# A one-element activation ahead of five waiting activations on ScalarE, in a float32 kernel of cross-attention and a gated MLP

## The chip, the cores and the metric

One Trainium2 chip, of which the kernel uses one core. The core has five engines with an instruction stream each: TensorE (PE in the profile, with its weight loads as PEld), VectorE (DVE), ScalarE (ACT), GpSimd (POOL) and SyncE (SP), the last two used here to start DMA transfers. The engines run side by side and wait for each other through semaphores. The metric is the device time of one execution in microseconds (us); lower is better. Inputs and outputs are float32 or float64 arrays in the device's memory (HBM), and the whole computation is one launch.

## The reference

Eight batches of eight heads attend in both directions between 512 tokens and 32 states; the two results are joined into 4352 rows of 512 and go through a gated MLP of width 2048.

```python
B, H, S, Ns, D = (8, 8, 512, 32, 64)            # x: (B,H,S,D)  state: (B,H,Ns,D)
scores = scale * x @ state^T;   a  = softmax(scores, -1);   xread = a  @ state
scores2 = scale * state @ x^T;  a2 = softmax(scores2, -1);  sread = a2 @ x
attn = concatenate([xread, sread], axis=2)      # (B, H, S + Ns, D)
x = attn.transpose(0, 2, 1, 3).reshape(B * (S + Ns), H * D)        # 4352 x 512
h = x @ w_in                                    # 4352 x 2048
sp = np.maximum(h, 0.0) + np.log1p(np.exp(-np.abs(h)))             # softplus
g = h * erf(sp)
return (g @ w_out).astype(np.float32)           # 4352 x 512
```

## The kernel before

Everything stays in float32. The MLP's input is never formed for the tokens: since xread is a @ state, `mixed` (line 841; `mixed0` at 602 for batch 0) multiplies the states of a batch by a part of w_in first, and `first_product` (935) multiplies the result by the transposed attention weights, which gives h transposed. The width of 2048 is worked in two halves (u = 0, 1), the tokens one batch at a time. `first_product` and `second_product` (1020) use seven block products in place of eight with sums of blocks around them (`seven`, 909), and `twice_product` (1123) does so at two levels. Those sums are DVE's work.

Between the two products stands the gate. For each of four blocks of h, ACT copies the block from PSUM into a large buffer called `ring` (line 961) or DVE adds it there (963, 967); ACT makes softplus of it (`soft`, line 971; 633 for batch 0; 1424 for the states), then erf (`serf`, line 986; 638; 1431), and DVE multiplies (989) and makes sums (1000). Attention itself needs the exponential on ACT (`attend`, lines 750 and 753). Softplus, erf and exponential need different function tables on ACT; the table is changed by an instruction of its own, ACT_TABLE_LOAD, which the compiler puts in wherever the next activation needs another table than the one at hand. There are 53 of them in the program. Copies run with any table.

The kernel doesn't issue instructions as it meets them. Each step is recorded with `op(engine, cost, at, go, reads, writes, table, ...)` (line 140), where `go` issues the instructions and `table` names the ACT table, if any. The order on each engine is then written out by hand in `ORDER` (177 to 298), as numbers of the recorded steps of that engine. `emit` (304) walks these five lists with a small model of costs (a change of table is 1.41 there, line 328) to interleave the engines, and calls the `go` of each step in the resulting order; `in_order` (78) then fixes that order on every engine. The waits follow from the data: the framework adds to each instruction the semaphores that it must wait for.

An instruction carries one wait. Where an activation must wait for two engines, the framework puts a separate instruction (EVENT_SEMAPHORE in the trace) ahead of it for the other one. In the built program the table load, where one is needed, stands directly ahead of the activation: ahead of the activation's own wait, and behind the separate one. Five of the 53 loads have such a separate wait ahead of them, all for DVE:

- the 4th load, of the softplus in line 633 (first half of batch 0), and the 8th, of the softplus in the same line (second half);
- the 10th, of the exponential in line 753 (batch 1);
- the 25th, of the softplus in line 971, and the 32nd, in the same line.

The fixed small tiles come from the pool `const`, first in the list of pools; `x`, `xq` (xin), `xT`, `sc` (att), `aT`, `sy` (keep), `m`, `sx` (mix), `raw` (act), `ot` and `oo` (outs) lie in pools that are allocated behind it.

Of the kernel before, what the change touches and what calls it, by code (L numbers as in the profile page):

```python
# [9 lines left out]
F32 = mybir.dt.float32  # L10
U32 = mybir.dt.uint32
ALU = mybir.AluOpType
ACTF = mybir.ActivationFunctionType
# [4 lines left out]
def kernel(  # L18
# [17 lines left out]
    nc = tc.nc  # L36
# [3 lines left out]
    P = 128  # L40
# [11 lines left out]
    const = ctx.enter_context(tc.tile_pool(name="const", bufs=1))  # L52
# [84 lines left out]
    PE, ACT, DVE, SP, GP = "tensor", "scalar", "vector", "sync", "gpsimd"  # L137
    ops, wrote, seen = [], {}, {}

    def op(engine, cost, at, go, reads=(), writes=(), table=None, land=0.0, pipe=0.0):  # L140
        n = len(ops)
        needs = set()
        for r in reads:
            needs.update(wrote.get(r, ()))
        for r in writes:
            needs.update(wrote.get(r, ()))
            needs.update(seen.get(r, ()))
        for r in reads:
            seen.setdefault(r, []).append(n)
        for r in writes:  # L150
            wrote[r], seen[r] = [n], []
        ops.append((engine, cost, at, go, needs, table, land, pipe))
# [5 lines left out]
    def either(name, cost, out, in_, at, reads, writes, by=None, run=None):  # L158
# [15 lines left out]
        else:  # L174
# [122 lines left out]
            36 39 35 38 42 37 44 40-41 43 46-47 52 45 48 55-56 49-50 53 57 51 54 59-60 63-64 61 65  # L297
            58 62 66 70 67 73 69 71 68 72 75 74 77 76 78 80 79 81 83 82""",
    }
    STARTS = {PE: 0.78, ACT: 0.74, DVE: 1.0, SP: 0.74, GP: 1.0}  # L300
    LAG = {PE: 0.24, ACT: 0.16, DVE: 0.17, SP: 0.2, GP: 0.2}
    FIXED, AHEAD = 2.5, 4.0

    def emit():

        mine = {e: [n for n, o in enumerate(ops) if o[0] == e] for e in LAG}
        queue = {}
        for e, text in ORDER.items():
            runs = [[int(k) for k in run.split("-")] for run in text.split()]
            queue[e] = deque(mine[e][k] for r in runs for k in range(r[0], r[-1] + 1))  # L310
            assert sorted(queue[e]) == mine[e]
        free, begin, end, piped = dict(STARTS), {}, {}, 0.0
        loaded = {ACT: None, PE: None}
        while any(queue.values()):
            ready = []
            for e, line in queue.items():
                if line and all(m in end for m in ops[line[0]][4]):
                    n = line[0]
                    ready.append((max([free[e]] + [end[m] + LAG[ops[m][0]] * (
                        ops[m][0] != e or ops[m][7] > 0) for m in ops[n][4]]), n, e))  # L320
            begun, n, e = min(ready)
            queue[e].popleft()
            begin[n] = begun
            _, cost, _, _, _, table, land, pipe = ops[n]
            if e == PE and table != loaded[PE]:
                cost, loaded[PE] = cost + (0.1 if table else 0.26), table
            elif e == ACT and table not in (None, loaded[ACT]):
                cost, loaded[ACT] = cost + 1.41, table
            end[n] = free[e] = begun + cost
            if pipe:  # L330
                piped = max(piped, begun) + pipe
                end[n] = max(piped, free[e]) + (land or FIXED)
                if e == SP:
                    free[e] = max(free[e], piped - AHEAD)
        order = sorted(begin, key=lambda n: (begin[n], n))
        for n in order:
            ops[n][3]()

    def adopt(names, into):

        every = [*names, *into]
        used = sorted({n for r in every for n in [*wrote.get(r, ()), *seen.get(r, ())]})
        for r in every:
            wrote[r], seen[r] = used, []
# [998 lines left out]
    def sums_states(u, at):  # L1343

        def part(j, k):
            return lambda: of_group[2 * u + j][:, :, 2 * k:2 * k + 2, :]

        def spare(k):
            return (mt(3) if k else static["aT0"]).rearrange("p e (i k f) -> p (e i) k f", k=2,
                                                             f=P)  # L1350

        def s4():
            return kept_tile("sx", lambda: mix.tile([P, 3, gw], F32, name="sx", bufs=1))[:, 0:2] \
                .rearrange("p e (i k f) -> p (e i) k f", k=2, f=P)

        def s3():
            return (static["xT"][:, 0:2] if u else oo()[:, 0]).rearrange(
                "p e (i k f) -> p (e i) k f", k=2, f=P)

        def get(n):  # L1360
            (X11, X12), (X21, X22) = ([part(j, k) for k in range(2)] for j in range(2))
            return (X11, X12, s4, X22, lambda: spare(0), lambda: spare(1), s3, X21)[n - 1]()

        block[u] = get

        of_j = [["w_in%d%d" % (u, j)] for j in range(2)]
        name = {1: of_j[0], 2: of_j[0], 3: ["sx0", "sx1"], 4: of_j[1],
                5: aT_of(0), 6: [("mS", 1, 0), ("mS", 1, 1)],
                7: ["xT0", "xT1"] if u else ["oo00", "oo01"], 8: of_j[1]}
        for o, x_, y_, how in ((5, 8, 4, ALU.add), (6, 5, 1, ALU.subtract), (7, 1, 8, ALU.subtract),  # L1370
                               (3, 2, 6, ALU.subtract)):
            op(DVE, 1.14, at, lambda o=o, x_=x_, y_=y_, how=how: tt(get(o), get(x_), get(y_), op=how),
               name[x_] + name[y_], name[o])
        return name
# [10 lines left out]
    def sums_reads(at):  # L1385

        def sub(o, x_, y_):
            v = views_s()
            tt(v[o - 1], v[x_ - 1], v[y_ - 1], op=ALU.subtract)

        turned = ["sT%d" % b for b in range(B)]
        for o, x_, y_ in SUMS_Y:
            op(DVE, 0.335, at, lambda o=o, x_=x_, y_=y_: sub(o, x_, y_),
               turned + [Y_s[x_ - 1], Y_s[y_ - 1]], [Y_s[o - 1]])
# [196 lines left out]
    for b in range(1, B):  # L1591
# [22 lines left out]
        def after(base, b=b):  # L1614
            if b == B - 1:
                for j, (k, used) in enumerate((
                        ("x", parts(0, 2) + parts(0, 3)),
                        ("xq", ["xq%d" % i for i in range(NI)] + [("Y", 0, 0, m) for m in sums]))):

                    def bring_in(j=j, k=k):  # L1620
                        flat = static[k].rearrange("p a b c -> p (a b c)")
                        of_group[2 + j] = flat.rearrange("p (j k f) -> p j k f", k=NK, f=P)
                        nc.sync.dma_start(out=flat.rearrange("p (j k) -> p j k", j=GF),
                                          in_=kept_in[:, GF * j:GF * j + GF])

                    op(SP, 0.5, base + 4, bring_in, [("kin", GF * j + f) for f in range(GF)],
                       [k, "w_in1%d" % j] + used, pipe=2.7)
                adopt([("Y", 0, 1, m) for m in sums], [("mS", 1, 0), ("mS", 1, 1)])
                adopt(parts(0, 0), ["oo00", "oo01"])
                names[0] = sums_states(0, base - 8)  # L1630
                sums_reads(base - 6)
# [49 lines left out]
    for n, b in enumerate(turns):  # L1681
# [13 lines left out]
        unit(b, 1, base + 34.5 * n, 0, hq[b], follow, between)  # L1695

    emit()
    in_order(begun)

# [29 lines left out]
```

## Time and profile before

| | |
|---|---|
| median of 3 runs | 696.99 us (696.93 to 697.43) |
| the profiled execution, by its own time | 696.16 us |
| its span, from the first instruction to the last | 694.3 us |
| TensorE clock granted, mean | 0.999 |
| ACT busy | 480.1 us, 850 instructions |
| ACT_TABLE_LOAD | 53, 1283 ns each |
| L971 softplus, 128 x 512 | 120, 631 ns each |
| DMA | 92.87 MB, 134 GB/s on average |

In a row of a group of instructions, the numbers after the bar are the busy time in us, the mean duration of one in ns, and the idle time of the engine just before them with what ended it. In a timeline, the columns are start and duration in us, engine, line, operation, tiles, shapes and count, and in brackets the idle time ahead with its releaser. The chain of waits is the work that ended last, followed back from the end; "issue" in it is time in which nothing that the profile shows was waited for. An engine's name with a q is its instruction queue.

### The profile page before, as it was taken

To read this page: it belongs to the slowest core of one execution; us is meant where nothing else is said; L and a number is where in the kernel's file an instruction comes from. 1 tells how busy PE (TensorE), PEld (TensorE's weight loads), DVE (VectorE), ACT (ScalarE), POOL (GpSimd) and SP (SyncE) were. 2 spreads that over 40 slices of the span, in tenths; PEclk is the share of its full clock that TensorE was granted. 3 is DMA by queue.
4 is the path that set the end of the run, shared out by engine and by line. 5 is a ranking of instruction groups with operands and counts; after the bars stand their busy time and mean duration, and the time that the engine had idled before them with its cause. 6 is when DMAs were issued, how large, how long until landed. Compare 5 with 4: busy or idle time off the path is not lost.

```text
span 694.3 us, 13176 instructions
## 1 busy us (share of the span) xinstructions
PE 686.8 (99%) x5193; PEld 584.0 (84%) x5193; DVE 581.7 (84%) x899; ACT 480.1 (69%) x850; POOL 85.8 (12%) x93
## 2 busy tenths in 40 slices
PE   9999999999999999999999999999999999999997
PEld 8435678787878788889998879898989898989997
DVE  5999899998989799989945779785969586949897
ACT  6987998988886695747255574848574857477742
POOL 0001000010001110000100000024101331312312
PEclk9999999999999999999999999999999999999999
DMA  9847976977889517425454302436322663721675
GB/s 266 231 141 177 180 233 155 216 199 187 287 171 276 169 49 267 125 84 152 119 157 166 84 1 61 122 42 119 46 69 31 118 89 71 105 31 18 89 138 107
DMA packets 133741, 92.87 MB, mean 134 GB/s; under 512 B 93744, under 2 KB 120752, under 8 KB 133168
## 3 DMA queue, kind: packets, MB, share of 16 engines
q1 hardware_dynamic: 113648, 61.29, 32.3%
q0 software_dynamic: 18800, 29.63, 22.8%
q10 hardware_dynamic: 1232, 1.11, 0.5%
q8 instruction: 41, 0.67, 0.4%
q14 instruction: 20, 0.16, 0.1%
HBM read 50.86 MB, written 41.16 MB: 133 GB/s over the span
## 4 chain that ended last, share of the span: by engine, by line
PE 93%; DVE 4%; ACT 1%; DMA 1%; issue 1%; SPq 0%; DVEq 0%; ACTq 0%
PE o L1270 31%; PE h L949 18%; PE o L1033 16%; PE at L949 7%; PE o L651 4%; PE o L1454 4%; PE h L1405 3%; PE h L850 2%; PE at L850 2%; PE at L626 1%; PE at L1405 1%; DVE ring L1000 1%; PE at L811 1%; PE h L718 1%; DMA x<-in_x_dram 1%; PE o L115 1%
## 5 line engine op out<-in xcount | busy, mean ns | idle before, releaser
L961 ACT COPY ring<-h 128x512 f32<-128x512 f32 x120 | 69.4, 586 | 70.9 <-PE h L949 66.3
L989 DVE TENSOR_TENSOR ring<-ring 128x1024 f32<-128x1024 f32 (+1 forms) x64 | 72.9, 1151 | 24.9 <-ACT ring L986 24.3
L949 PE MATMUL h<-aT,m 128*128 128x256 f32 x360 | 92.0, 380 | 0.0
L971 ACT ACTIVATE ring<-ring 128x512 f32<-128x512 f32 x120 | 72.2, 631 | 10.8 <-DVE ring L967 4.9
L1033 PE MATMUL o<-w_out,ring 128*128 128x256 f32 x320 | 77.1, 381 | 0.0
L1000 DVE TENSOR_TENSOR ring<-ring 128x1024 f32<-128x1024 f32 x60 | 72.6, 1217 | 0.4
L949 PEld LDWEIGHTS h<-aT,m 128*128 128x128 f32 x360 | 65.3, 190 | 8.5 <-issue 1.0
L1033 PEld LDWEIGHTS o<-w_out,ring 128*128 128x128 f32 x320 | 59.9, 190 | 13.1 <-issue 2.5
L1270 PE MATMUL o<-w_out,w_in 128*128 128x128 f32 x512 | 68.7, 275 | 0.0
L1270 PEld LDWEIGHTS o<-w_out,w_in 128*128 128x128 f32 x512 | 64.3, 192 | 1.5
L1270 PE MATMUL o<-w_out,ring 128*128 128x128 f32 x480 | 64.7, 275 | 0.6 <-ACT oo L1280 0.6
L1270 PEld LDWEIGHTS o<-w_out,ring 128*128 128x128 f32 x480 | 60.6, 192 | 3.0 <-ACT oo L1280 1.0
L986 ACT ACTIVATE ring<-ring 128x1024 f32<-128x1024 f32 (+1 forms) x64 | 62.8, 1007 | 0.2
L1033 PE MATMUL o<-raw,ring 128*128 128x256 f32 x240 | 58.9, 380 | 0.0
L1033 PEld LDWEIGHTS o<-raw,ring 128*128 128x128 f32 x240 | 45.1, 190 | 7.1 <-issue 0.8
L1270 PE MATMUL o<-raw,ring 128*128 128x128 f32 x360 | 49.5, 275 | 0.0
L1270 PEld LDWEIGHTS o<-raw,ring 128*128 128x128 f32 x360 | 46.1, 192 | 2.0 <-DVE sc L1285 0.8
L1270 PEld LDWEIGHTS o<-raw,xT 128*128 128x128 f32 x320 | 38.8, 192 | 3.7 <-ACT o L1301 2.5
L1270 PE MATMUL o<-raw,xT 128*128 128x128 f32 x320 | 41.5, 277 | 0.0
L1189 POOL DMA_DIRECT2D out_dram<-oo x16 | 23.0, 1526 | 126.0 <-ACT x L1280 62.3
L949 PE MATMUL h<-sy,sx 128*128 128x256 f32 x120 | 31.4, 385 | 0.8 <-ACT h L919 0.8
L949 PE MATMUL h<-sy,m 128*128 128x256 f32 x120 | 31.1, 382 | 0.0
(269 smaller groups left out, 1398.8 us busy)
## 6 DMA issues: line engine op xcount, KB each, us to landing
x<-in_x_dram SPq DMA_DIRECT2D x30, 256.0 KB, 5.0
xq<-in_x_dram SPq DMA_DIRECT2D x112, 64.0 KB, 2.6
out_dram<-oo SPq DMA_DIRECT2D x10, 512.0 KB, 3.9
raw<-in_moe_w_in_dram SPq DMA_DIRECT2D x8, 512.0 KB, 6.5
raw<-in_moe_w_out_dram SPq DMA_DIRECT2D x4, 1024.0 KB, 6.2
raw<-in_moe_w_in_dram POOLq DMA_DIRECT2D x8, 512.0 KB, 6.5
raw<-in_moe_w_out_dram POOLq DMA_DIRECT2D x8, 512.0 KB, 5.5
kept_a<-aT SPq DMA_DIRECT2D x8, 512.0 KB, 4.5
```

The lines of the kernel that those rows point to most:

```text
L651: nc.tensor.matmul(out=bank("o%d" % r), lhsT=gT[g][:, i, P * r:P * r + P], rhs=w_out[:, GF * g + i, :], start=(made_of[r] == 1), stop=(mad ...
L850: nc.tensor.matmul(out=bank(names[k])[Ns * p:Ns * p + Ns, :], lhsT=st[r, b, q], rhs=of_group[2 * u + j][r, :, i, :], start=True, stop=True)
L949: nc.tensor.matmul(out=out_[:, i], lhsT=x_[:, q:q + P], rhs=y_, start=(start and i == 0), stop=(i == 1), skip_group_check=not start)
L961: op(ACT, 0.5, t, lambda: nc.scalar.copy(out_(), view(bank(name))), [name], w)
L971: op(ACT, 0.53, t, lambda: nc.scalar.activation(out=part(splane, k), in_=part(hplane, k), func=ACTF.Softplus), area(hplane, ks=[k], os=[o] ...
L986: op(ACT, 0.085 + 0.875 * share, at + n, lambda s_=s_: nc.scalar.activation(out=s_, in_=s_, func=ACTF.Erf), [], area(splane, ks=[k], os=os ...
L989: op(DVE, 0.065 + 1.075 * share, at + n + 1, lambda s_=s_, h_=h_: tt(s_, s_, h_, op=ALU.mult), area(hplane, ks=[k], os=os), area(splane, k ...
L1000: op(DVE, 1.14, at + k, lambda k=k, x_=x_, y_=y_, how=how: tt(get("h", k), get(*x_), get(*y_), op=how), area(v[x_[0]], ks=[x_[1]]) + area( ...
L1033: nc.tensor.matmul(out=view(name)[:, h], lhsT=lhs[:, i, :], rhs=weight_of[n]()[:, u, i, :], start=(start and h == 0 and i == 0), stop=(h = ...
L1270: nc.tensor.matmul(out=out_[:, Q2 * k:Q2 * k + Q2], lhsT=lhs[:, k, i], rhs=rhs[:, i], start=first, stop=(k == len(ns) - 1 and i == 1), ski ...
L1405: nc.tensor.matmul(out=bank(bk)[:, P * i:P * i + P], lhsT=x_[:, i, k], rhs=y_[:, k], start=(start and i == 0 and k == 0), stop=(i == GF - ...
L1454: nc.tensor.matmul(out=bank("o%d" % bk)[:, E2 * c:E2 * c + E2], lhsT=ring[:, w_[w], plane, k][:, i, :], rhs=weight_of[n]()[:, u, i, :], st ...
```

## The change

A tile `spark` of one element per partition is added to `const`. After the order is found, `emit` goes through it, counts the changes of table on ACT, and at the 4th, 8th, 10th, 25th and 32nd wraps the step's `go`: it first issues an activation of the same function on a constant, one element per partition, written to `spark`, and then what it issued before. That activation reads nothing that is computed and so waits for nothing; it now is the first to need the table. In the built program each of these five loads stands directly ahead of it, with the separate wait and the old activation behind. There are 53 loads as before and five activations more; the order of all other instructions on every engine is the same.

```diff
+    EARLY = {4, 8, 10, 25, 32}
+    spark = const.tile([P, 1], F32, name="spark")
+
+    def ahead(n):
+        func = {"softplus": ACTF.Softplus, "erf": ACTF.Erf, "exp": ACTF.Exp}[ops[n][5]]
+        go = ops[n][3]
+
+        def after():
+            nc.scalar.activation(out=spark, in_=nc.const_aps.tensor(1.0, [P, 1], F32), func=func)
+            go()
+
+        ops[n] = (*ops[n][:3], after, *ops[n][4:])
+
     STARTS = {PE: 0.78, ACT: 0.74, DVE: 1.0, SP: 0.74, GP: 1.0}
...
         order = sorted(begin, key=lambda n: (begin[n], n))
+        loaded, loads = None, 0
+        for n in order:
+            table = ops[n][5]
+            if ops[n][0] == ACT and table not in (None, loaded):
+                loaded, loads = table, loads + 1
+                if loads in EARLY:
+                    ahead(n)
         for n in order:
             ops[n][3]()
```

## The prediction

> **What bounds the kernel now.** I read the busy shares first, then the chain that ended last, then what TensorE (PE) waited for, and last the two stretches in which it waited for ScalarE (ACT).
>
> ```profile
> PE 686.8 (99%) x5193; PEld 584.0 (84%) x5193; DVE 581.7 (84%) x899; ACT 480.1 (69%) x850; POOL 85.8 (12%) x93
> ...
> PE 93%; DVE 4%; ACT 1%; DMA 1%; issue 1%; SPq 0%; DVEq 0%; ACTq 0%
> ```
>
> PE is busy for 99% of the span and is 93% of the chain, at a full clock. A change on ACT can only buy time in which PE stands still, so next comes the complete list of PE's waits (engine, line, what ended the wait; us in total, times, longest):
>
> ```profile
> PE h L949 <- ACT h L919: 0.8, 1, 0.8
> PE o L115 <- PEq L1713: 0.8, 1, 0.8
> PE o L1270 <- ACT oo L1280: 0.6, 1, 0.6
> PE o L421 <- DMA x<-in_x_dram: 0.4, 1, 0.4
> PE o L1270 <- ACT ot L1280: 0.2, 1, 0.2
> ```
>
> Two of the five belong to the start of the program and the last is far from any edit. What can be won is the first and the third. The chain around the first (start us, us, what):
>
> ```profile
> 222.19 0.60 DVE ring L963
> 222.79 0.02 issue
> 222.81 0.02 ACTq L971
> 222.83 0.03 issue
> 222.86 0.42 ACT L971
> 223.28 0.87 issue
> 224.15 0.63 ACT ring L971
> 224.78 0.48 ACT ring L961
> 225.27 0.02 issue
> 225.29 0.58 ACT h L919
> 225.87 0.04 issue
> 225.91 1.13 PE h L949 x4
> ```
>
> ACTq is ACT's instruction queue finishing a separate wait for VectorE (DVE). Only then does the table load run (222.86, shown as "ACT L971" and the issue behind it), then the softplus of L971, two copies, and PE. The load is paid after the wait, on the chain. ACT's own order of time around the third wait, and around the first edit:
>
> ```profile
> 304.01 0.27 ACT L1280 COPY ot<-o 128x128 f32<-128x128 f32 x1
> 305.14 1.28 ACT L971 ACT_TABLE_LOAD   x1 [0.85 <-DVE ring L1000]
> 306.43 0.63 ACT L971 ACTIVATE ring<-ring 128x512 f32<-128x512 f32 x1
> 306.97 0.63 ACT L1280 COPY oo<-o 128x256 f32<-128x256 f32 x2
> ...
> 26.98 1.28 ACT L633 ACT_TABLE_LOAD   x1
> ```
>
> At 305.14 it is the same picture with a shorter idle time ahead (0.85 us); at 26.98 no bracket follows the load, so ACT came to it without a pause and the wait ahead of it was over.
>
> **The change part by part.** Five loads (the 4th, 8th, 10th, 25th and 32nd of 53; in the trace at 26.98, 49.58, 56.44, 222.86 and 305.14) move ahead of their DVE wait, each followed by a new activation on one element per partition. No wait and no DMA is added or moved; the orders of PE, DVE, SP and POOL stay.
>
> *The new activation.* The trace has none of this size. ACTIVATE in L986 takes 622 ns for 512 elements and 1062 for 1024, so 0.859 ns an element, and 622 - 511 x 0.859 = 183 ns for one; the next instruction starts some 93 ns before an activation ends (ACT's copy at 224.69 starts while the softplus of 224.15 + 0.63 = 224.78 still runs), so its slot is 0.09 us. Bounds: 0 (it vanishes in the load's shadow) and 0.31 (the 308 ns of the smallest ACTIVATE, L168 on 64 elements, with no overlap). I take 0.09; the one-element read of an accumulator (190 ns, L753) stands nearest to it.
>
> *Load at 222.86.* ACT has been idle for 4.16 us, since 218.70. Load (1.28) and activation then end at about 220.2, long before the DVE result of 222.79. The softplus starts at 222.86 instead of 224.15, 1.29 earlier. The copy of L961 behind it needs a PE product whose end ACT's queue saw at 223.28; it would start at 223.40 and is not held up. The copy of L919 ends at 225.86 - 1.29 = 224.57. PE's previous work, eight matmuls of L1033 from 223.18 at 0.216 us each (the chain has x8 in 1.73), lets the next one start at 224.91; it started at 225.91. So PE no longer waits: 1.00 saved, 0.3 us of the ACT gain unused. After the pause the four matmuls needed 0.97 until the next ones start at 226.88, against 4 x 0.216 = 0.86; this 0.11 should go with it. Sum -1.1; bounds -0.84 (the idle time alone) and -1.11.
>
> *Load at 305.14.* ACT is free at 304.28. The load runs 304.30 to 305.59, the new activation to 305.78, and the softplus can start at 305.69 instead of 306.43: -0.74. Its DVE wait (305.07) is then over. The copies of L1280 shift with it, and PE restarts at 306.91 instead of 307.65; without any wait it could at 305.98 + 4 x 0.216 = 306.85. So -0.74; bounds -0.52 (an activation of 0.31 without overlap) and -0.90 (no pause at all, with its 0.1 restart).
>
> *Load at 26.98.* It cannot start earlier, so the new activation is pure cost. Behind it stand the softplus of L633 and the conversion of L561 (28.77); DVE's L565 follows the latter, then DVE's copy of L164 (30.55), and PE's matmul at 31.29 waits for that (its weight load has been idle for 0.71, released by DVE's st L164; it starts 0.90 after the matmul pair of 30.38, where two at 0.43 need 0.86). So +0.09; bounds 0 and +0.31.
>
> *Loads at 49.58 and 56.44.* The first again starts without a pause: ACT is 0.09 later until the 1.14 us of idle time ahead of the second, which swallow it. The second load moves into that idle time (55.30), and the exponential of L753 starts about 1.0 earlier. PE runs twenty matmuls of L651 from 51.56 and nothing but work up to 65 us, so neither is worth anything: 0. Without that cover the first would cost 0.09 and the second gain up to 1.0.
>
> *What could be late next.* From 225.91 to 307 PE has no idle time, and DVE has 6.1 us of waits between 226 and 300, all for ACT or PE. The wait of 305.07 itself hangs on PE: product at 299.98, copy L961, DVE L963, L1252, L1000 twice. So DVE and ACT follow an earlier PE, and I let the 1.1 stand at 305.
>
> *A page against the trace.* Each of the 53 loads lasts 1283 ns, starts some 18 ns after the instruction before it where nothing holds it, and its activation starts 11 ns after its end. The Trainium skill (ScalarE: Activation LUTs, What ACT_TABLE_LOAD costs) puts about 1380 ns of drain on top, 2.66 us a switch. The trace agrees with its load and shows no drain. By the page, as an estimate, the moved load of 305.14 would hold the softplus until 304.30 + 2.66 + 0.01 + 0.09 = 307.06, 0.63 later than now, and the sum would be -1.1 + 0.63 + 0.09 = -0.4.
>
> *Sum.* -1.1 - 0.74 + 0.09 = -1.75 us. The profiled execution took 696.16, of which 694.3 is the span and 1.86 lies around it; its span should become 692.55. The median shown is 696.99, 0.83 above the profiled execution, and I take the difference off that: 695.25. With all bounds at one end: -0.84 - 0.52 + 0.31 = -1.05 (695.95) and -1.11 - 0.90 = -2.0 (695.0).
>
> **The rivals.**
> 1. *The lead is lost before 305.* If DVE does not follow PE, the wait at 305.07 stays where it is, PE only arrives earlier at the same closed gate, and the gate opens 0.74 earlier thanks to the second load: -0.74 + 0.09 = -0.65, 696.3. For it: DVE is busy 24.5 of 25 us in 250 to 275. Against: the 6.1 us of DVE waits for PE and ACT.
> 2. *The loads do not profit.* Where the load's place or its switch costs something that these rows hide, both gains vanish: 697.0 to 697.1. For it: the load of 222.86 came only after the wait, though ACT had 4.16 us. Against: that load stood behind a separate wait in ACT's stream, and the built program now has it ahead of that wait. Elsewhere a load does run ahead of its activation's own wait: at 39.81 to 41.09, with the activation of L633 at 41.92.
> 3. *The drain of the page*: a load that keeps ACT for 2.66 us gives 696.6. No load of the trace has it.
> 4. *Slower: the tile.* The new tile takes 32 bytes of every partition, and x, xq, xT, sc, aT, sy, m, sx, raw, ot and oo, allocated behind it, all start 32 bytes later. At least 840 (L949) + 240 (L1033 on raw) + 968 (L1270 on raw, m or xq) + 448 (L811) = 2496 PE records have an operand there. If each cost one column more (216 / 256 = 0.84 ns) that is 2.1 us, 697.3; two columns 4.2 us, 699.4. From 1.75 / 2496 = 0.70 ns a record on it decides. For it: no row shows an operand of PE at such a start in steady work, and PE has no slack. Against: operands in w_out and in raw, whose starts in the partition differ by an odd multiple of 64 bytes, cost the same (381 and 380 ns in L1033, 275 and 275 in L1270).
>
> **How the numbers follow.** Forecast 0.70 at 695.25; lead lost 0.11; loads without profit 0.05; drain 0.03; slower tile 0.11. A measurement of this kernel can tell about 0.2% from no change, 1.4 us, so "faster" begins at 695.6. The forecast's own range, 695.0 to 695.95, lies mostly below that: I give 0.60 of its 0.70 to faster and 0.10 to the same, with rivals 1 to 3 (0.19) and 0.02 of rival 4; the other 0.09 of rival 4 is slower. The range is 694.7 to 696.7: the forecast with its bounds and 0.3 for a median of few runs, rivals 1 and 3; rivals 2 and 4 (0.16) are left out.
>
> **What would show it.** In the profile after: the list of PE's waits without ACT h L919, and ACT oo L1280 at 0.1 or less; a load right behind the copy that ends at 218.7 (less what came before), followed by an activation of about 0.18 on one element; the softplus of L971 right behind its wait; 53 loads still; the five new activations at 180 to 310 ns. Rival 1 is right if the wait for ACT oo L1280 is as long as now or longer; rival 4 if matmuls of L949 are more than 216 ns apart. I am wrong if PE waits as before while the loads stand early, or if a new wait of PE of some tenths turns up.

## The result and the profile after

The changed kernel takes 694.80 us (median of 8 runs, 694.52 to 695.93) against 696.96 for the one before in as many runs (696.01 to 697.43). The ratio is 0.9973 with an interval of 0.9962 to 0.9983: 1.9 us less, 1.2 to 2.65 by the interval (the two medians lie 2.16 apart). The profiled execution took 694.83, its span 693.0, against 694.3 before.

The page after, busy shares and the shares of the chain by engine:

```profile
PE 686.7 (99%) x5193; PEld 583.9 (84%) x5193; DVE 581.8 (84%) x899; ACT 481.2 (69%) x855; POOL 85.8 (12%) x93
...
PE 92%; ACT 3%; DVE 2%; issue 1%; DMA 1%; DVEq 0%; ACTq 0%; POOLq 0%
```

The five new activations are there (ACT 855 instructions instead of 850, 1.1 us more busy), and PE's work is the same. The complete list of PE's waits after, read as before:

```profile
PE o L115 <- PEq L1733: 0.8, 1, 0.8
PE h L969 <- ACT sc L744: 0.4, 1, 0.4
PE at L646 <- DVE m L164: 0.3, 1, 0.3
PE o L1290 <- ACT ot L1300: 0.2, 1, 0.2
```

Lines have moved: L949 is now L969, L971 is L991, L919 is L939, L1270 is L1290, L1280 is L1300, L724 is L744, L563 is L583. The two waits that the prediction wanted gone (for ACT h and for ACT oo) are gone. Two others have come that were not there, of 0.4 and 0.3 us, and the prediction had named a new wait of some tenths as a sign that it is wrong. ACT in order of time around the load that stood at 222.86:

```profile
218.69 0.59 ACT L981 COPY ring<-h 128x512 f32<-128x512 f32 x1
219.30 1.28 ACT L308 ACT_TABLE_LOAD   x1
220.59 0.20 ACT L308 ACTIVATE spark<-const-float32-1.0 128x1 f32<-128x1 f32 x1
222.96 0.63 ACT L991 ACTIVATE ring<-ring 128x512 f32<-128x512 f32 x1 [2.16 <-DVE ring L983]
...
224.10 0.57 ACT L939 COPY h<-h 128x512 f32<-128x512 f32 x1
```

The load stands 0.02 us behind the copy, the one-element activation 0.01 behind the load, and ACT then waits 2.16 us for DVE with its table at hand. The softplus follows its wait, and the copy that PE needs ends at 224.67 instead of 225.87. PE in order of time there:

```profile
223.26 1.89 PE L1053 MATMUL o<-raw,ring 128*128 128x256 f32 x8
224.99 1.03 PE L969 MATMUL h<-sy,sx 128*128 128x256 f32 x4
```

The four matmuls follow the eight without a pause (1.73 us for eight, as before). And ACT at the load that stood at 305.14:

```profile
303.63 0.27 ACT L1300 COPY ot<-o 128x128 f32<-128x128 f32 x1
303.92 1.28 ACT L308 ACT_TABLE_LOAD   x1
305.22 0.20 ACT L308 ACTIVATE spark<-const-float32-1.0 128x1 f32<-128x1 f32 x1
305.32 0.61 ACT L991 ACTIVATE ring<-ring 128x512 f32<-128x512 f32 x1
```

No bracket any more: ACT works without a pause from the copy to the softplus.

To see where the time came from I matched all 5193 matmuls of the two traces in order and took the difference of their starts, after minus before: +0.08 us at 60, -1.03 behind 226, -0.38 behind 250, -1.12 behind 308, -1.25 at the end. So the first load brought 1.11, the second 0.74, and 0.65 was given back at 250, where the new wait for ACT sc L744 stands. ACT ahead of that place, after:

```profile
242.50 0.67 ACT L583 ACTIVATE raw<-raw 128x512 uint32<-128x512 uint32 x1 [0.85 <-DMA raw<-in_moe_w_out_dram]
```

and the same instruction before:

```profile
242.55 0.69 ACT L563 ACTIVATE raw<-raw 128x512 uint32<-128x512 uint32 x1
```

Before, the block of w_out had landed when ACT came to its conversion of it; after, ACT waited 0.85 us for it. Whether the change caused that, and whether the loads did the rest, is what the experiments ask. "Theory A" in their expectations is the prediction's account: the gain is made by the 25th and the 32nd load and by nothing else.

### The profile page after: what moved, and what is told of

The parts are those of the page before. It is cut to its first block, busy times and chain, and to the rows that moved or that the text cites. A ratio compares the mean times of both kernels' runs of the same rounds, so it can differ in the third digit from the quotient of the medians.

```text
span 693.0 us, 13181 instructions
## 1 busy us (share of the span) xinstructions
PE 686.7 (99%) x5193; PEld 583.9 (84%) x5193; DVE 581.8 (84%) x899; ACT 481.2 (69%) x855; POOL 85.8 (12%) x93
## 3 DMA queue, kind: packets, MB, share of 16 engines
q10 hardware_dynamic: 1232, 1.11, 0.5%
## 4 chain that ended last, share of the span: by engine, by line
PE 92%; ACT 3%; DVE 2%; issue 1%; DMA 1%; DVEq 0%; ACTq 0%; POOLq 0%
PE o L1290 31%; PE h L969 19%; PE o L1053 16%; PE at L969 8%; PE o L1474 4%; PE h L1425 3%; PE o L671 2%; PE h L870 2%; PE at L870 2%; PE o L115 1%; PE at L1425 1%; PE at L831 1%; DMA raw<-in_moe_w_out_dram 1%; PE h L738 1%; PE at L646 1%
## 5 line engine op out<-in xcount | busy, mean ns | idle before, releaser
L969 PE MATMUL h<-aT,m 128*128 128x256 f32 x360 | 92.1, 380 | 0.4 <-ACT sc L744 0.4
L991 ACT ACTIVATE ring<-ring 128x512 f32<-128x512 f32 x120 | 72.2, 631 | 13.0 <-DVE ring L987 4.9
L969 PEld LDWEIGHTS h<-aT,m 128*128 128x128 f32 x360 | 65.2, 190 | 9.2 <-issue 1.0
L1290 PE MATMUL o<-w_out,w_in 128*128 128x128 f32 x512 | 68.7, 275 | 0.0
L1290 PEld LDWEIGHTS o<-w_out,w_in 128*128 128x128 f32 x512 | 64.3, 192 | 1.5
L1290 PE MATMUL o<-w_out,ring 128*128 128x128 f32 x480 | 64.7, 275 | 0.0
L1290 PEld LDWEIGHTS o<-w_out,ring 128*128 128x128 f32 x480 | 60.6, 192 | 2.3 <-issue 0.8
L1290 PE MATMUL o<-raw,ring 128*128 128x128 f32 x360 | 49.5, 275 | 0.0
L1290 PEld LDWEIGHTS o<-raw,ring 128*128 128x128 f32 x360 | 46.1, 192 | 2.0 <-DVE sc L1305 0.8
L1290 PEld LDWEIGHTS o<-raw,xT 128*128 128x128 f32 x320 | 38.7, 192 | 3.7 <-ACT o L1321 2.5
L1290 PE MATMUL o<-raw,xT 128*128 128x128 f32 x320 | 41.3, 276 | 0.0
L969 PE MATMUL h<-sy,sx 128*128 128x256 f32 x120 | 31.3, 384 | 0.0
L969 PE MATMUL h<-sy,m 128*128 128x256 f32 x120 | 31.1, 382 | 0.0
```

Source lines behind the costliest of these rows:

```text
L969: nc.tensor.matmul(out=out_[:, i], lhsT=x_[:, q:q + P], rhs=y_, start=(start and i == 0), stop=(i == 1), skip_group_check=not start)
L991: op(ACT, 0.53, t, lambda: nc.scalar.activation(out=part(splane, k), in_=part(hplane, k), func=ACTF.Softplus), area(hplane, ks=[k], os=[o] ...
L1290: nc.tensor.matmul(out=out_[:, Q2 * k:Q2 * k + Q2], lhsT=lhs[:, k, i], rhs=rhs[:, i], start=first, stop=(k == len(ns) - 1 and i == 1), ski ...
```

## The experiments

### One load at a time

The set of loads with an activation ahead is cut to one, to the first three, or to the two that should matter; nothing else differs. All four ran on one chip, where the kernel before took 696.47 (33 runs).

```diff
-    EARLY = {4, 8, 10, 25, 32}
+    EARLY = {25}             # second_only
+    EARLY = {32}             # third_only
+    EARLY = {4, 8, 10}       # first_three
+    EARLY = {25, 32}         # two_only
```

*second_only*

> Only the 25th load (at 222.86 in the profile before) is moved ahead of its wait. Theory A (the gain is PE's pauses): PE's wait for ACT h L919 is gone and PE is 1.1 us ahead at 226; in the profile of the changed kernel 0.65 of such a lead was given back at 250, where ACT had waited for a load of raw, so -0.5 to -1.1 us in all, 695.9 to 696.5 against 696.96; the wait of about 0.64 for ACT oo at 307 is there as before. Theory B (what counts is the 32 bytes by which the tile moves all later tiles): the whole gain of about 2 us, since the tile is there. Theory C (nothing but scatter between runs): no difference.

Measured 695.89 us, ratio 0.9988 (0.9979 to 0.9997). PE's waits, the complete list:

```profile
PE o L115 <- PEq L1733: 0.8, 1, 0.8
PE o L1290 <- ACT oo L1300: 0.6, 1, 0.6
PE o L1290 <- ACT ot L1300: 0.2, 1, 0.2
```

*third_only*

> Only the 32nd load (at 305.14) is moved. Theory A: PE's wait for ACT oo L1280 is gone or below 0.1, the wait of 0.84 for ACT h L919 at 225 stays; -0.74 us, 696.2. Theory B: the whole gain of about 2 us. Theory C: no difference.

Measured 696.28 us, ratio 1.0000 (0.9991 to 1.0009). The 0.74 expected would be a ratio of 0.9989, just outside this interval: by its time alone this run is a miss. PE's waits, the complete list:

```profile
PE h L969 <- ACT h L939: 0.8, 1, 0.8
PE o L115 <- PEq L1733: 0.8, 1, 0.8
PE o L1290 <- ACT ot L1300: 0.2, 1, 0.2
PE at L646 <- DVE m L164: 0.2, 1, 0.2
```

*first_three*

> Only the 4th, 8th and 10th loads are moved. Theory A: no gain and +0.1 us from the new activation behind the 4th load, if the work after it has no room by 46 us, 697.0 to 697.1; both waits for ACT at 225 and 307 as before. Theory B: the whole gain of about 2 us, 695. Theory C: no difference.

Measured 697.08 us, ratio 1.0006 (0.9997 to 1.0015), 0.6 above the kernel before by the medians where 0.1 was expected; the interval holds both. Of PE's waits:

```profile
PE h L969 <- ACT h L939: 0.8, 1, 0.8
PE at L646 <- DVE m L164: 0.8, 1, 0.8
...
PE o L1290 <- ACT oo L1300: 0.6, 1, 0.6
```

*two_only*

> Only the 25th and the 32nd loads are moved. Theory A: the gain of the whole change and up to 0.1 us more, -1.2 to -1.9 us against before (694.8 to 695.7); neither wait for ACT is left. Theory B: the same as the whole change, about -2. Theory C: no difference.

Measured 695.46 us, ratio 0.9986 (0.9978 to 0.9995): 1.0 below the kernel before, where 1.2 to 1.9 were expected. Of PE's waits, those that the list of before doesn't have:

```profile
PE h L969 <- ACT sc L744: 0.5, 1, 0.5
PE o L671 <- DVE ring L662: 0.4, 1, 0.4
PE at L646 <- DVE m L164: 0.3, 1, 0.3
```

Each edit takes away its own wait and leaves the other: with the 25th alone only the wait for ACT h goes, with the 32nd alone only that for ACT oo, with the first three both stay, with the two both go. Matmul by matmul the gain is the same in every trace that has the edit, 1.11 at 226 and 0.74 at 307. The times resolve this badly: the 0.74 of third_only doesn't show in its ratio, and two_only came out nearer to second_only than to the whole change. Three of the four traces also carry delays that these two places don't explain, in the first 46 us and at 250 (in third_only 0.62 and 0.36, which is more than its gain); these are taken up below.

### What of the activation matters, and where its tile lies

Four kernels on a second chip, the kernel before at 696.49 us (26 runs). The first is the change unaltered.

> The changed kernel once more, unchanged, beside the others of this group. Theory A (PE's pauses, with a lead that a late load of raw may eat up to 0.8 us of at 250): -1.0 to -1.9 us against before, near the -1.0 of the kernel with only the 25th and 32nd loads moved. If the first three loads bring something of their own, it stays at -2 us. In its profile: 1.1 less at 226, 0.74 less at 307; the start of the program, up to 46 us, scatters by up to 1.8 us between profiles whatever the kernel.

Measured 694.55 us, ratio 0.9973 (0.9962 to 0.9984).

The second takes the tile out of `const` and into a pool allocated behind all the others, so that x, xq, raw and the rest lie where they lay before:

```diff
+    last = ctx.enter_context(tc.tile_pool(name="last", bufs=1))   # behind outs
...
-    spark = const.tile([P, 1], F32, name="spark")
+    spark = last.tile([P, 1], F32, name="spark")
```

> The whole change, but the small tile lies in a pool behind all others, so no other tile moves by 32 bytes. Theory A: the same as the whole change in this group within 0.5 us. Theory B (the moved tiles cost or bring something): another time than the whole change in this group, slower if moved tiles bring part of its gain, faster if they cost.

Measured 694.54 us, ratio 0.9971 (0.9960 to 0.9981), beside 0.9973 with the shift. The 32 bytes cost nothing that can be seen here.

The third keeps the five activations, their place and their tile, and gives them a function that runs with any table, so that each load stays behind its wait:

```diff
-        func = {"softplus": ACTF.Softplus, "erf": ACTF.Erf, "exp": ACTF.Exp}[ops[n][5]]
+        func = ACTF.Copy
```

> The five new activations are there, but as copies, which need no table: the five loads stay behind their waits. Theory A: no gain, 0 to +0.2 us; both of PE's waits for ACT, 0.84 at 225 and 0.64 at 307, are there. If the tile's place or the new activation itself made the gain, -1 to -2 us.

Measured 696.77 us, ratio 0.9998 (0.9990 to 1.0007). ACT in order of time at the 25th load:

```profile
219.76 0.20 ACT L308 ACTIVATE spark<-const-float32-1.0 128x1 f32<-128x1 f32 x1
223.62 1.28 ACT L991 ACT_TABLE_LOAD   x1 [3.66 <-DVE ring L983]
224.91 0.63 ACT L991 ACTIVATE ring<-ring 128x512 f32<-128x512 f32 x1
```

The activation runs as early as in the changed kernel, the load comes 3.66 us later behind the wait, and PE has both of its old waits:

```profile
PE h L969 <- ACT h L939: 0.8, 1, 0.8
...
PE o L1290 <- ACT oo L1300: 0.6, 1, 0.6
```

So the whole gain is the place of the load, and none of it the activation.

The fourth tests the wait at 250. My reading then was that PE's lead starts the fetch of `raw` in worse company, beside other transfers, and that the lead is eaten by it. Of the last block of 128 rows of w_out only the first 128 of 512 columns are fetched, so that the transfer is shorter (its output is made with what `raw` holds in the other columns); the loads are those of two_only.

```diff
-            out=half(k, h)),
-            in_=moe_w_out[P * f:P * f + P].bitcast(U32)),
+            out=half(k, h)[:, :256 if f == NF - 1 else None],
+            in_=moe_w_out[P * f:P * f + P, :128 if f == NF - 1 else None].bitcast(U32)),
```

> The 25th and 32nd loads are moved; besides, of the last of the eight later blocks of w_out only the first 128 of 512 columns are fetched (line 551, the transfer of raw that starts near 237 and that ACT's conversion at 242.5 waits for), so that part of w_out is wrong and the transfer is a quarter. Theory D (a transfer of raw that does not land earlier eats the lead at 250): no wait of PE for ACT sc at 250, the lead of 1.1 us from 226 is whole at 305 and 1.85 after 307; -1.5 to -1.9 us. Rival R (ACT's own work, not the transfer, is late there): a wait of 0.4 to 0.5 for ACT sc at 250 remains, and -1.0 us in all.

Measured 695.15 us, ratio 0.9982 (0.9973 to 0.9990): 1.3 below the kernel before, between what theory D (1.5 to 1.9) and the rival (1.0) expected, so its time doesn't decide. The transfer took 3.45 us instead of 5.89 in the changed kernel's profile, and ACT's conversion starts without a pause:

```profile
242.31 0.70 ACT L584 ACTIVATE raw<-raw 128x512 uint32<-128x512 uint32 x1
```

PE has no wait at 250, and its lead of 1.11 arrives whole at 307, where 0.74 is added. That fits a lead that is lost through this transfer, but one profile can't carry it: f_two, below, keeps its lead with the whole transfer. The table below decides that. That the lead itself makes the transfer late doesn't follow in either case.

### Do the first three loads matter, and how far does one kernel scatter

By then the change with all five stood at 0.9973, 0.9973 and 0.9971, but two_only at 0.9986, on different chips. Four sets on one chip, the kernel before at 696.62 us (24 runs):

```diff
+    EARLY = {4, 8, 10, 25, 32}    # f_all
+    EARLY = {25, 32}              # f_two
+    EARLY = {4, 8, 25, 32}        # f_four_eight
+    EARLY = {10, 25, 32}          # f_ten
```

> The change as it is, all five activations, beside the other three of this call on the same chip. Theory A (only the loads before the 25th and 32nd switch bring anything; what lies ahead of 46 us scatters from execution to execution): 1.0 to 1.9 us below before, and level with the kernel of two to within 0.4 us. Rival (the first three loads bring something of their own, some 0.7 us, which the single profiles hide): 1.9 below before and 0.7 or more below the kernel of two.

> Activations ahead of the 25th and 32nd load alone, once more. Theory A: level with all five to within 0.4 us, 1.0 to 1.9 below before. Rival of the first three: 1.0 below before, 0.7 or more above all five.

> Activations ahead of the loads 4, 8, 25 and 32. Theory A: the slot ahead of the erf at 27 us costs 0.1 at most, so level with the kernel of two to within 0.4. Rival of the first three: if the gain is with 4 or 8, as low as all five; if it is with 10, as high as the kernel of two.

> Activations ahead of the loads 10, 25 and 32. Theory A: level with the kernel of two to within 0.4. Rival of the first three: as low as all five if the gain is with 10, as high as the kernel of two if it is with 4 or 8.

| | median | ratio | interval |
|---|---|---|---|
| all five | 694.90 us | 0.9977 | 0.9968 to 0.9986 |
| 25, 32 | 694.47 us | 0.9972 | 0.9961 to 0.9982 |
| 4, 8, 25, 32 | 694.97 us | 0.9976 | 0.9967 to 0.9985 |
| 10, 25, 32 | 694.62 us | 0.9971 | 0.9959 to 0.9982 |

All four agree within their intervals, and f_two is not above f_all, so the rival that the first three loads bring something falls. The two with the 4th and 8th stand 0.28 to 0.50 us above the two without, inside the intervals, though two of these differences are over the 0.4 that was expected at most; no version here is shown to be better than the change as it was made.

PE's waits in f_two, the complete list:

```profile
PE o L115 <- PEq L1733: 0.8, 1, 0.8
PE o L1290 <- ACT ot L1300: 0.2, 1, 0.2
```

This is the same kernel as two_only, without three of its waits. Its ACT at the place of the give-back:

```profile
241.62 0.69 ACT L583 ACTIVATE raw<-raw 128x512 uint32<-128x512 uint32 x1
```

With the whole lead PE had no wait here: the fetch took 4.71 us this time. The table compares the fetch in all profiles but that of short_fetch. It has PE's start differences to the profile of before, in us: the level at 60 us, the steps at 226, 250 and 307, and, from the trace's issue and landing, how long the fetch of `raw` from w_out took that ACT needs at 242.

| profile | level at 60 | step at 226 | step at 250 | step at 307 | fetch took |
|---|---|---|---|---|---|
| before | 0 | | | | 4.36 |
| first_three | +1.84 | 0 | 0 | 0 | 4.25 |
| copy_ahead | +0.75 | 0 | 0 | 0 | 4.66 |
| third_only | +0.62 | 0 | +0.36 | -0.74 | 5.59 |
| second_only | +0.24 | -1.11 | 0 | 0 | 4.76 |
| f_all | +1.10 | -1.11 | 0 | -0.74 | 4.24 |
| f_four_eight | +1.60 | -1.11 | 0 | -0.74 | 4.40 |
| f_two | +0.18 | -1.11 | 0 | -0.74 | 4.71 |
| tile_behind | +0.74 | -1.11 | +0.10 | -0.74 | 5.34 |
| f_ten | -0.10 | -1.11 | +0.16 | -0.74 | 5.39 |
| after | +0.08 | -1.11 | +0.65 | -0.74 | 5.89 |
| two_only | +1.15 | -1.11 | +0.78 | -0.74 | 6.02 |
| whole_again | +0.19 | -1.10 | +0.90 | -0.74 | 6.12 |

What is lost at 250 is the fetch's time less 5.24 us, to 0.02, wherever it takes longer than that, and nothing elsewhere (5.59 - 5.24 = 0.35 for third_only, 6.12 - 5.24 = 0.88 for whole_again). It holds without the lead too: third_only has PE's old wait at 226 and loses 0.36. The bound doesn't move because the fetch is issued behind a result of DVE that comes earlier with the lead (issued at 237.56 before, at 236.53 after). So 0.65 was lost in the profile of after because the fetch took 5.89 us in this execution, and not because it was issued at the wrong time. Whether the lead makes a slow fetch more likely is not shown: with the 25th load moved five of nine took longer than 5.24 us, without it one of four, too few to tell. My reading ahead of short_fetch, worse company, finds no support: in f_four_eight a block of w_in was still on its way until 1.46 us behind the issue and the fetch took 4.40, in whole_again that block had landed before the issue and it took 6.12.

Why one transfer takes 4.2 us in one execution and 6.1 in the next stays open, but the kept traces narrow it down. Its landing is marked by 16 updates of a semaphore. In all thirteen profiles 15 of them are in by 4.34 us behind the issue; only the last scatters, from 4.24 to 6.12. Each profile also has one packet of 16 KB of the kind "instruction", 0.9 us long, in these microseconds: in that of after from 3.72 to 4.68 behind the issue, and a packet of 4 KB follows it at 4.66. That it holds up the last part where that is late is a candidate and not shown, as the trace doesn't tell which of the 16 DMA engines a packet ran on.

Three small steps are not in the table: +0.22 near 170 in tile_behind, -0.16 at 479 in every profile against that of before, and +0.16 at 397 in the profiles with the 25th and 32nd alone (f_two, two_only, short_fetch). I know no cause for the last.

The level at 60 us scatters in the same way. In f_four_eight, ACT in order of time:

```profile
35.62 1.14 ACT L581 ACTIVATE w_in<-raw 128x1024 f32<-128x1024 f32 x1
37.59 1.17 ACT L583 ACTIVATE raw<-raw 128x1024 uint32<-128x1024 uint32 x1 [0.84 <-DVE ring L662]
```

The DVE result named in the bracket was done at 37.04; the block of w_in that this instruction reads landed at 37.52. It is again a transfer: issued at 32.11, 5.41 us, once one before it, that took 7.54, had landed at 32.00. In f_two it landed at 34.98, and the same instruction starts at 36.02 without a pause. PE pays at 46, in the wait for DVE m L164. All seven kernels with an activation at the 4th load lose 0.19 to 0.99 there, but two_only, short_fetch and third_only lose 0.31 to 0.47 without one, so no edit is needed for it. As it is all of the seven and only three of the six others, the runs don't exclude that the activation adds to it.

## Why the prediction was right

**What bounds the kernel.** That only PE's pauses can be won, and that the list of its waits holds two that hang on a load, was right: what the profiles with both edits gained at those places is the first wait with its restart and the second but for 0.06 us: in f_two the matmul at the second place starts 0.28 us after the one ahead of it, where 0.22 is the distance without a pause and 1.02 was that of before.

**The load at 222.86.** Predicted -1.1 with bounds of -0.84 and -1.11; -1.10 or -1.11 in all ten profiles that have the edit. The steps came out one by one: the next matmul was to start at 224.91 and did at 224.99, the +0.08 being the level of that execution. The 0.3 of ACT's gain that PE can't use was lost as worked out.

**The load at 305.14.** Predicted -0.74, measured -0.74 or -0.75 in all ten profiles that have the edit. Put back by the 0.38 that PE then led, load and softplus start at 304.30 and 305.70; predicted were 304.30 and 305.69. The 0.06 of a pause that is left is in the prediction too (306.91 against 306.85).

**The load at 26.98.** Predicted +0.09, by way of the conversion of w_out on DVE to the matmul at 31.29. That matmul is 0.05 to 0.10 later in all seven kernels with an activation there and in none of the others. The medians of the last four would allow 0.5. What comes on top at 46 hangs on a transfer, so I can't tell 0.1 from 0.5 as the price in the time: the mechanism of this term is shown, its size in the time is not.

**The loads at 49.58 and 56.44.** Predicted 0: in first_three no matmul between 60 and 470 us is earlier relative to its level. The load at 56.44 did move by more than a microsecond, under PE's work.

**The activation.** 203 ns, not 183, and a slot of 0.10 to 0.11 (305.22 to 305.32), not 0.09; too little to matter, and within the bounds:

```profile
26.49 1.28 ACT L308 ACT_TABLE_LOAD   x1
27.78 0.20 ACT L308 ACTIVATE spark<-const-float32-1.0 128x1 f32<-128x1 f32 x1
27.89 0.58 ACT L653 ACTIVATE ring<-at 128x512 f32<-128x512 f32 x1
```

**What could be late next.** "I let the 1.1 stand at 305" held in five of the ten profiles with the lead (one of them with the shortened fetch) and failed by 0.10 to 0.90 in the other five. This is the step that the prediction had wrong. I had looked for the next gate on DVE and ACT, and it was a DMA: before, the fetch of w_out for `raw` had 0.63 us to spare, landing at 241.92 for an instruction at 242.55, and I didn't ask how steady a transfer is. The prediction named a new wait of PE of some tenths as a sign against it; in the profile of after it was there (0.4 for ACT sc L744 at 250, and 0.3 for DVE m L164 at 46). f_two has neither with the same lead, and third_only, which has no lead at 250, loses 0.36 there, so it can come without the lead.

**The rivals.** *Lead lost before 305*: a loss is there in some executions, but by a transfer and not by DVE, and the gate at 305 follows PE: f_two has -1.11 and -0.74 one upon the other. *Loads without profit*: refuted by the traces of each single edit. *The drain of the page*: the load at 303.92 holds the softplus until 305.32, 1.40 us with the activation's slot in it. The 2.66 us a switch of the Trainium skill (ScalarE: Activation LUTs, What ACT_TABLE_LOAD costs) would, as an estimate, have held it until 306.7. The sum by that page of the skill, -0.4, is outside the interval. *The tile*: its forecast of 2 us more than the change alone is refuted by the result itself, and tile_behind shows no difference (0.9971 against 0.9973).

**The number.** The steps at the three places, -1.11, -0.74 and +0.08, make -1.77, against -1.75 forecast. The profile of after has four more that the prediction doesn't have: -0.47 before 30 us, +0.47 at 46, +0.65 at 250 and -0.16 at 479. The first two cancel by luck, and its span stands 0.45 above the forecast of 692.55. f_two, without the activation at 26.98 and without a slow fetch, has 692.6, with 0.18 lost in the start. The median of 694.80 is 0.45 below the 695.25, and just below the 695.0 of all bounds together; it lies in the range because that allowed another 0.3 for a median of few runs. Medians differ by as much without an edit: f_two and two_only are one kernel and came out at 694.47 and 695.46 on two chips, 2.15 and 1.01 below the kernel before.

## What to carry to other kernels

Where an activation needs another table and waits for two engines, look at which side of the wait its table load stands; a one-element activation of the same function on a constant ahead of it moves the load into the idle time, for a tenth of a microsecond, and is worth it only where PE waits behind that activation. When gains are a few tenths of a per cent, match the instructions of two traces and read the steps: 1.11 and 0.74 came out the same in every trace while the medians of one kernel differed by 1 us. Before laying a step in the trace to an edit, look for the same step in a kernel without it.

## What the runs showed of the hardware

One transfer, unchanged in size and issuing queue, took between 4.24 and 6.12 us in thirteen executions, with 15 of its 16 parts landed within 4.34 us each time, and the kernel feels whatever goes beyond 5.24. Together with the transfers of the first 40 us this makes two profiled executions of one kernel differ by 1.8 us in their spans (two_only 694.4, f_two 692.6: 0.97 by 60 us, 0.78 at 250), as much as the change brings. A table load with no wait ahead of it costs nothing but itself here: 1283 ns, with 0.02 us or less ahead of it and 0.01 behind.
